# Counting SyncE's issues anew in a planner that orders attention and a feed-forward network

## The chip, the cores and the metric

The kernel runs on one core of one Trainium2 chip. The metric is the device time of one execution in microseconds; three runs before the change gave 1017.01, 1020.22 and 1020.98 us, a median of 1020.22 us. A core has a matrix engine (TensorE, "PE", which loads weights in "PEld"), three engines for elementwise work (VectorE "DVE", ScalarE "ACT", GpSimd "POOL"), and SyncE ("SP"), which in this kernel does nothing but issue DMA transfers, one after the other, and wait for what each of them needs. All of them run their own instruction stream in order and meet at semaphores.

## The reference

```python
# q, k, v: (8 batches, 8 heads, 576 rows, 64), s: (8, 8, 576)
scores = scale * np.matmul(q, k.transpose(0, 1, 3, 2))
cum = np.cumsum(np.maximum(s, 0.0), axis=-1)
bias = -(cum[:, :, :, None] - cum[:, :, None, :])
scores = np.where(causal, -1000000000.0, scores + np.minimum(bias, 0.0))
attn = softmax(scores)                       # row maximum taken off, 1e-9 in the sum
x = (attn @ v) laid out as (4608 tokens, 512)
h = x @ w_in                                 # 512 -> 2048
g = np.where(h > 0.0, h, np.exp(np.minimum(h, 0.0)) - 1.0)
out = g @ w_out                              # 2048 -> 512
```

Causal attention with a bias that decays along the sequence, and behind it a two-layer network with an ELU between the layers.

## The kernel before

**Attention** goes through the heads in pairs (two heads of one batch). The first 320 rows of the first three batches are computed directly in float32 ("low" units). The rest is done with pairs of float16 parts: queries and keys are loaded (`stq`, `stk`), split into a high and a low part (`parts`), written to DRAM (`spread`), and read back in the layout that the score matmuls want (`set`). For each block of 128 queries the scores come out of PE (`sc`, L1141), DVE adds the mask and takes the row minimum (L1144), ACT takes the exponential (L1149), and the weights are scaled and split into float16 parts (L1201 to L1209). A transposed DMA load turns them (`T<-p`, issued on SP by `turned_load`, L481), and the `av` matmuls (L1328) multiply them with the values. A head with four query blocks issues four transposed loads of 4, 6, 8 and 9 blocks of 128 x 128 elements; a head with two blocks issues one joint load, of 9 blocks for the early rows and of 17 for the late ones. The results are written to `x_dram`.

**The feed-forward network** goes through the 4608 tokens in 18 chunks of 256. A chunk's rows are loaded from `x_dram` (`xc`) and split (`xh`, `xl`); the first layer makes `h` (L1503), ACT and DVE make ELU of it (L1515 to L1542), and the second layer adds up `o` (L1560). The first chunk is in float32. The weights are loaded, measured and split in the first part of the run. During the first 60 us PE is kept running with matmuls that nobody reads (`scratch`, the "fillers").

**What sets the order of the work.** The kernel states its operations with what each reads and writes, and a planner (`Plan`) writes out the order at build time. `Plan.run` simulates the five engines: each operation has one or more ways (an engine, a cost in ns, the instructions); of the operations that are ready, the one that can start first names the engine, and on that engine the operation with the earliest due date is taken among those that can start then. The chosen way depends on when the engines come free. A transfer costs SP its issue time and lands later: a fixed lag of 4000 ns, and its bytes at 285 bytes per ns on one shared pipe. `Plan.deadlines` walks the finished order backwards from its end and gives each operation the latest moment at which it could have been done; `Plan.issue` repeats the simulation with those as due dates and keeps the order whose simulated end is earliest. The first round has no due dates and goes by the priorities written in the code. What is kept is then written out, instruction by instruction, and is the order of each engine's queue on the chip. Nothing is chosen anew at run time: an engine waits for its next instruction even where a later one could go.

The issue costs on SP that the simulation uses stand in three constants: `SP_COST` for plain transfers, `SP_SHORT` for the loads and stores around `stq`, `stk`, `spread` and `set`, and `SP_TURN` per block of a transposed load, with a floor in `turned_load`.

Of the kernel before, what the change touches and what calls it, by code (L numbers as in the profile page):

```python
# [35 lines left out]
LAG, RATE = 4000.0, 285.0  # L36
# [6 lines left out]

N_CUT, CUT, N_LOW = 4, 2, 3
PRIO_LOW = 10
SP_COST, SP_SHORT, SP_TURN = 500.0, 640.0, 170.0

N_FREE = 0

# [42 lines left out]


class Op:
    __slots__ = ("ways", "after", "before", "behind", "bufs", "new", "prio", "ready", "left", "filler", "late", "at", "frees")


class Plan:
# [45 lines left out]
    def op(self, prio, ways, reads=(), writes=(), late=()):  # L144

        o = Op()
        o.ways, o.prio, o.filler = ways, (prio, len(self.ops)), False
        o.after, o.before, o.behind, o.bufs, o.new = set(late), [], [], set(), []
        firsts = set()
        for accesses, write in ((reads, False), (writes, True)):  # L150
            expanded = []
            for a in accesses:
                b, part = a if isinstance(a, tuple) else (a, None)
                if not isinstance(b, Piece):
                    expanded.append((b, part))
                elif part is None:
                    known = [key for key in b.whole.parts if key is not None and key[0] == b.label]
                    expanded += [(b.whole, key) for key in known or [(b.label, None)]]
                else:
                    expanded.append((b.whole, (b.label, part)))  # L160
            for b, part in expanded:
                if not b.parts and b not in o.bufs:

                    o.new.append((b, self.place(b)))
                    b.first = o
                firsts.add(b.first)
                if b not in o.bufs:
                    o.bufs.add(b)
                    b.used_by.append(o)
                for key, (writers, readers) in b.parts.items():  # L170
                    if part is None or key is None or key == part:
                        o.after.update(writers)
                        if write:
                            o.after.update(readers)
                writers, readers = b.parts.setdefault(part, ([], []))
                if write:
                    if part is None:
                        b.parts = {None: ([o], [])}
                    else:
                        b.parts[part] = ([o], [])  # L180
                else:
                    readers.append(o)
        o.after.discard(o)
        firsts -= o.after | {o}
        for d in o.after:
            d.before.append(o)
        for d in firsts:
            d.behind.append(o)
        o.left, o.ready, o.late = len(o.after) + len(firsts), {}, 0.0
        self.ops.append(o)  # L190
        return o

# [18 lines left out]
    def deadlines(self, order, end):  # L211

        late = dict.fromkeys(self.ENDS, end)
        for o in reversed(order):
            engine, start, stop, lag = o.at
            t = late.get(engine, end)
            for d in o.before:
                if d.at is not None:
                    t = min(t, d.late - lag - self.HOPS.get((engine, d.at[0]), self.HOP))
            for b in o.bufs:  # L220
                for d in b.followed:
                    t = min(t, d.late - lag - self.HOPS.get((engine, d.at[0]), self.HOP))
            t -= stop - start
            for d in o.behind:
                if d.at is not None:
                    t = min(t, d.late)
            o.late = t
            if engine in late:
                late[engine] = t

    ENDS = ("PE",)
    ROUNDS, WAIT = 8, {"PE": 0.0, "DVE": 0.0, "ACT": 0.0, "Pool": 0.0, "SP": 0.0}

    def issue(self):
        best = None
        for n in range(self.ROUNDS):
            self.reset()
            self.wait = n > 0
            end, order = self.run(False)
            if best is None or end < best[0]:  # L240
                best = end, self.wait, [(o, o.late) for o in self.ops]
            self.deadlines(order, end)
        _, self.wait, lates = best
        for o, late in lates:
            o.late = late
        self.reset()
        return self.run(True)

    def run(self, emit):
# [5 lines left out]
        order = []  # L255
# [6 lines left out]
        def slot_free(key, bufs):  # L262

            held = slots.get(key, ())
            if len(held) < bufs:
                return {}
            was = held[-bufs]
            return None if was.users else was.until
# [5 lines left out]
        while pending:  # L274
# [13 lines left out]
            for o in pending:  # L288
                slots_free = []
                for b, k in o.new:  # L290
                    at = None
                    if b.home_bufs and taken[b.home] == k:
                        b.key, b.bufs = b.home, b.home_bufs
                        at = slot_free(b.key, b.bufs)
# [22 lines left out]
            until, engine = first[0] + (self.WAIT[first[2]] if self.wait else 0.0), first[2]  # L317
            start, _, _, n, o = min(
                (x for x in found if x[2] == engine and (x[0] <= until and not x[4].filler or x is first)),
                key=lambda x: (x[4].late, x[1]))  # L320
            if o.filler:
                start -= GAP
            engine, cost, trace = o.ways[n][:3]
# [1 line left out]
            end = start + cost  # L325
# [36 lines left out]
            at = len(block.instructions)  # L362
# [65 lines left out]
def kernel(  # L428
# [23 lines left out]
    nc = tc.nc  # L452
# [19 lines left out]
    op = plan.op  # L472
    act, dve, pool, pe_ = nc.scalar, nc.vector, nc.gpsimd, nc.tensor

    def load(prio, dst, src, reads, writes, nbytes, late=(), lag=LAG, cost=SP_COST):
        return op(prio, [("SP", cost, lambda: nc.sync.dma_start(dst(), src()), lag, nbytes)],
                  reads, writes, late)

    def turned_load(prio, units, dst, src, reads, writes):

        op(prio, [("SP", max(1330.0, SP_TURN * units), lambda: nc.sync.dma_start_transpose(dst(), src()), LAG,  # L481
                   units * P * P * 2.2)], reads, writes)

    def rounded(prio, n, dst, src, reads, writes, sign=1.0, only=None):

        ways = [
            ("Pool", pool_1(n),
             lambda: pool.tensor_scalar(dst(), src(), sign, 1.0, ALU.mult, ALU.mult)),
            ("ACT", act_s(n),
             lambda: act.activation(dst(), src(), AF.Copy, scale=sign)),  # L490
            ("DVE-SB", dve_1(n),
             lambda: dve.tensor_scalar(dst(), src(), sign, None, ALU.mult)),
        ]
        op(prio, [w for w in ways if only is None or w[0] in only], reads, writes)
# [675 lines left out]
    def halved(u, i, pt, sm, col):  # L1170
# [47 lines left out]
        if joint:  # L1218
            turned_load(prio, 2 * turns - 1, lambda: u.pt.v, lambda: t16.v, used, [u.pt])
        else:  # L1220
            turned_load(prio, turns, lambda: u.pt.v[:, at::n][:, :turns],
                        lambda: t16.v[:, base * P : (base + turns) * P], used, [(u.pt, i)])
# [421 lines left out]
    while rows:  # L1644
        chunk, left = [], TMAX
        while left:
            b, late, r, n = rows.pop(0)
# [82 lines left out]
```

## Time and profile before

| | before |
|---|---|
| median of three runs | 1020.22 us (1017.01 to 1020.98) |
| profiled execution | 1021.47 us, its span 1019.7 us |
| PE busy | 997.2 us (98%) |
| DVE, ACT, POOL busy | 846.5, 660.1 and 261.1 us |
| granted PE clock, mean | 0.998 |
| transfers of SP's queue | 178.45 MB, 76.6% of 16 engines' span |

The span runs from the first to the last instruction. "Busy" is the share of time in which an engine has at least one instruction under way; matmuls are pipelined, so that a busy PE need not run at its full rate. A wait is put down to what came last. In a timeline a row gives the start, the duration, the engine, the line of the kernel, the operation and what it writes and reads. "SPq" is SP's queue, and a duration there is the time that an issue took, not that of the transfer.

### The profile page before, as it was taken

To read this page: it belongs to the slowest core of one execution; us is meant where nothing else is said; L and a number is where in the kernel's file an instruction comes from. 1 tells how busy PE (TensorE), PEld (TensorE's weight loads), DVE (VectorE), ACT (ScalarE), POOL (GpSimd) and SP (SyncE) were. 2 spreads that over 40 slices of the span, in tenths; PEclk is the share of its full clock that TensorE was granted. 3 is DMA by queue.
4 is the path that set the end of the run, shared out by engine and by line. 5 is a ranking of instruction groups with operands and counts; after the bars stand their busy time and mean duration, and the time that the engine had idled before them with its cause. 6 is when DMAs were issued, how large, how long until landed. Compare 5 with 4: busy or idle time off the path is not lost.

```text
span 1019.7 us, 21777 instructions
## 1 busy us (share of the span) xinstructions
PE 997.2 (98%) x7327; PEld 686.5 (67%) x7327; DVE 846.5 (83%) x2352; ACT 660.1 (65%) x1583; POOL 261.1 (26%) x429
## 2 busy tenths in 40 slices
PE   8999999999989999999999999999999999999998
PEld 7677666666656666666666666666766666666665
DVE  6899899989989898999998998898979898744343
ACT  5999776776667676676776777666657665533232
POOL 6332272423232323322222222221412330100000
PEclk9999999999999999999999999999999999999999
DMA  7888743688999997899889999989979998521000
GB/s 205 251 256 274 208 130 87 133 224 162 195 205 205 225 224 178 191 223 214 184 181 225 199 185 203 239 185 240 189 177 217 204 210 180 92 69 43 1 22 21
DMA packets 296724, 179.83 MB, mean 176 GB/s; under 512 B 209908, under 2 KB 270564, under 8 KB 296612
## 3 DMA queue, kind: packets, MB, share of 16 engines
q1 hardware_dynamic: 296612, 178.45, 76.6%
q8 instruction: 57, 0.93, 0.4%
q14 instruction: 55, 0.45, 0.1%
HBM read 93.08 MB, written 36.81 MB: 127 GB/s over the span
## 4 chain that ended last, share of the span: by engine, by line
PE 45%; DVE 4%; DMA 2%; issue 1%; ACT 1%; SPq 0%; DVEq 0%; ACTq 0%
PE h L1503 19%; PE o L1560 19%; PE sc L1141 3%; PE av L1328 3%; DMA T<-p 1%; DVE p L1209 1%; DVE p L1144 1%; DMA stq<-in_qT_dram 0%; DVE gg L1542 0%; DVE h L1535 0%; DMA spread<-parts 0%; ACT p L1149 0%; DVE p L1203 0%; DVE parts L1064 0%; ACT g L1522 0%
## 5 line engine op out<-in xcount | busy, mean ns | idle before, releaser
L1503 PE MATMUL h<-xh,wp 128*128 128x256 f16 x2176 | 401.5, 273 | 0.0
L1560 PE MATMUL o<-wp,gg 128*128 128x512 f16 x1632 | 391.2, 379 | 4.1 <-DVE tops L723 1.5
L1503 PEld LDWEIGHTS <-wp 128*128 128x128 f16 x3264 | 317.4, 98 | 66.1 <-issue 1.3
L1503 PE MATMUL h<-xl,wp 128*128 128x256 f16 x1088 | 296.9, 273 | 0.0
L1560 PEld LDWEIGHTS <-gg 128*128 128x128 f16 x1632 | 156.8, 98 | 152.8 <-DVE gg L1542 5.9
L1149 ACT ACTIVATE p<-p,mn 128x192 f32<-128x192 f32 (+1 forms) x232 | 144.0, 621 | 80.1 <-DVE mn L1144 77.5
L1209 DVE SCALAR_TENSOR_TENSOR p<-p,sm,p 128x512 f16<-128x512 f32 (+3 forms) x258 | 155.1, 630 | 3.4 <-ACT p L1205 1.5
L1515 ACT ACTIVATE g<-h,cs 128x512 f32<-128x512 f32 x136 | 92.4, 679 | 77.1 <-PE h L1503 75.5
L1539 ACT ACTIVATE gg<-h 128x512 f16<-128x512 f32 x127 | 75.4, 593 | 85.5 <-DVE h L1535 84.7
L1542 DVE SCALAR_TENSOR_TENSOR gg<-h,gg 128x512 f16<-128x512 f32 x136 | 93.2, 685 | 25.0 <-ACT gg L1539 24.5
L1141 PE MATMUL sc<-set 128*128 128x288 f16 (+3 forms) x544 | 109.7, 298 | 2.9 <-DVE mn L1144 1.6
L1144 DVE CUSTOM_DVE_ANT_0 p<-sc,maskw 128x192 f32<-128x192 f32 (+1 forms) x232 | 108.6, 480 | 4.2 <-PE sc L1141 1.8
L1535 DVE SCALAR_TENSOR_TENSOR h<-g,cs,h 128x512 f32<-128x512 f32 x136 | 101.9, 749 | 9.1 <-ACT g L1522 5.2
L1201 POOL TENSOR_SCALAR p<-p,sm 128x512 f16<-128x512 f32 (+3 forms) x78 | 53.6, 691 | 217.6 <-DVE sm L1155 80.3
L1205 ACT ACTIVATE p<-p,sm 128x512 f16<-128x512 f32 (+3 forms) x152 | 79.1, 532 | 26.5 <-ACT p L1149 8.3
L1526 DVE TENSOR_SCALAR g<-g 128x512 f32<-128x512 f32 x81 | 36.3, 448 | 58.1 <-ACT g L1515 57.7
L1141 PEld LDWEIGHTS <-set 128*128 128x128 f16 x584 | 55.1, 98 | 35.8 <-issue 6.0
L1328 PEld LDWEIGHTS <-v 128*64 128x64 f16 x960 | 48.5, 111 | 24.4 <-issue 13.7
L1328 PE MATMUL av<-T,v 128*64 128x256 f16 (+5 forms) x960 | 62.3, 281 | 2.1 <-DMA T<-p 2.0
L500 POOL TENSOR_SCALAR v<-va,scales 128x320 f16<-128x320 f32 (+1 forms) x41 | 25.3, 620 | 98.7 <-PE av L1328 66.8
L500 POOL TENSOR_SCALAR xh<-xc,cs 128x512 f16<-128x512 f32 x22 | 16.7, 760 | 130.0 <-PE h L1503 127.0
L1149 ACT ACTIVATION_READ_ACCUMULATOR p<-p,mn 128x1 f32 x232 | 43.6, 188 | 0.0
(205 smaller groups left out, 1271.2 us busy)
## 6 DMA issues: line engine op xcount, KB each, us to landing
set<-spread SPq DMA_DIRECT2D x32, 432.0 KB
spread<-parts_None SPq DMA_DIRECT2D x32, 288.0 KB
set<-spread SPq DMA_DIRECT2D x32, 288.0 KB
raws<-in_w_in_dram SPq DMA_DIRECT2D x16, 512.0 KB
raws<-in_w_out_dram SPq DMA_DIRECT2D x16, 512.0 KB
out_dram<-ost SPq DMA_DIRECT2D x32, 256.0 KB
va<-in_vb_dram SPq DMA_DIRECT2D x16, 352.0 KB
xc<-x_dram SPq DMA_DIRECT2D x22, 256.0 KB
```

The costliest lines, as they stand in the source:

```text
L1141: pe_.matmul(view(sc.v[:, :cw]), l, r, start=n == 0, stop=n == len(pairs) - 1)
L1144: op(prio, [("DVE", 168 + cw + 55 * (i > 0), lambda i=i, sc=sc: dve.tensor_tensor_reduce(pt.v[:, i * cw : (i + 1) * cw], sc.v[:, :cw], mv( ...
L1149: op(prio, [("ACT", 383 + w / 1.2, lambda: act.activation(pt.v[:, :w], pt.v[:, :w], AF.Exp, bias=mn.v[:, n - 1 : n], scale=-1.0, accum_out ...
L1205: ("ACT", 295 + size / 1.2, lambda part=part: act.activation(part(0), own(part), AF.Copy, scale=sm.v[:, r])),
L1209: ("DVE-SB", dve_2(size), lambda part=part: dve.scalar_tensor_tensor(part(1), own(part), sm.v[:, r], part(0), ALU.mult, ALU.subtract)),
L1328: pe_.matmul(av.v[w.h * HB : (w.h + 1) * HB, dst], w.values.v[:, w.h, kb, v], part(w, kb, m), start=kb == 0 and m == 0 and v == 0, stop=kb ...
L1503: pe_.matmul(columns(k), weight_part(f, 0, part)[1]()[:, c * P : (c + 1) * P], xx.v[:, c], start=(c == 0 and m == 0), stop=(c == NCB - 1 a ...
L1515: op(side, [("ACT", act_c(W) + (0 if native else 90), lambda: act.activation(g.v, hp.v, AF.Exp, scale=1.0 if native else by(3)))], [hp] + ...
L1535: op(side, [("DVE", dve_p(W) + 60, lambda: dve.scalar_tensor_tensor(hp.v, g.v, by(2 if sign[0] else 1), hp.v, ALU.mult, ALU.max))], [g, cs ...
L1539: ("ACT", act_c(W), lambda: act.activation(gg.v[:, 0], hp.v, AF.Copy, scale=2.0**-DOWN)),
L1542: op(side, [("DVE", dve_p(W), lambda: dve.scalar_tensor_tensor(gg.v[:, 1], hp.v, 2.0**-DOWN, gg.v[:, 0], ALU.mult, ALU.subtract))], [hp, ( ...
L1560: pe_.matmul(acc[i].v, gg.v[:, g, at], weight_part(f, 1, part)[1](), start=(f == 0 and m == 0), stop=(f == NF - 1 and m == 2),)
```

## The change

Three constants of the planner get other values: the plain issue is counted at 520 ns instead of 500, the transposed load at 195 ns per block instead of 170, and its floor is 1440 ns instead of 1330. `SP_SHORT` stays at 640. The planner makes six rounds instead of eight. In the backward walk, successors that are fillers are left out, and the due date that the choice goes by is kept in a field of its own, `due`, which is copied from `late` after each walk. The operations, the engines that they may run on and SP as the one queue for transfers stay.

```diff
-SP_COST, SP_SHORT, SP_TURN = 500.0, 640.0, 170.0
+SP_COST, SP_SHORT, SP_TURN = 520.0, 640.0, 195.0
...
             for d in o.before:
-                if d.at is not None:
+                if d.at is not None and not d.filler:
                     t = min(t, d.late - lag - self.HOPS.get((engine, d.at[0]), self.HOP))
...
             for d in o.behind:
-                if d.at is not None:
+                if d.at is not None and not d.filler:
                     t = min(t, d.late)
...
-    ROUNDS, WAIT = 8, {"PE": 0.0, "DVE": 0.0, "ACT": 0.0, "Pool": 0.0, "SP": 0.0}
+    ROUNDS, WAIT = 6, {"PE": 0.0, "DVE": 0.0, "ACT": 0.0, "Pool": 0.0, "SP": 0.0}
...
             if best is None or end < best[0]:
-                best = end, self.wait, [(o, o.late) for o in self.ops]
+                best = end, self.wait, [(o, o.due) for o in self.ops]
             self.deadlines(order, end)
+            for o in order:
+                o.due = o.late
...
-                key=lambda x: (x[4].late, x[1]))
+                key=lambda x: (x[4].due, x[1]))
...
-        op(prio, [("SP", max(1330.0, SP_TURN * units), lambda: nc.sync.dma_start_transpose(dst(), src()), LAG,
+        op(prio, [("SP", max(1440.0, SP_TURN * units), lambda: nc.sync.dma_start_transpose(dst(), src()), LAG,
                    units * P * P * 2.2)], reads, writes)
```

More of the change, by code (lines that the diff above doesn't have):

```diff
@@ L94 @@
 class Op:
-    __slots__ = ("ways", "after", "before", "behind", "bufs", "new", "prio", "ready", "left", "filler", "late", "at", "frees")
+    __slots__ = ("ways", "after", "before", "behind", "bufs", "new", "prio", "ready", "left", "filler", "late", "at", "due")
 class Plan:
@@ L188, in op @@
             d.behind.append(o)
-        o.left, o.ready, o.late = len(o.after) + len(firsts), {}, 0.0
+        o.left, o.ready, o.due = len(o.after) + len(firsts), {}, 0.0
         self.ops.append(o)
@@ L240, in issue @@
             if best is None or end < best[0]:
-                best = end, self.wait, [(o, o.late) for o in self.ops]
+                best = end, self.wait, [(o, o.due) for o in self.ops]
             self.deadlines(order, end)
+            for o in order:
+                o.due = o.late
         _, self.wait, lates = best
-        for o, late in lates:
-            o.late = late
+        for o, due in lates:
+            o.due = due
         self.reset()
```

## The prediction

> **What bounds the kernel now.** I read the page's head and table of engines first, then the stretches, to see where TensorE (PE) is idle and what clock it had.
>
> ```profile
> span 1019.7 us, 21777 instructions
> PE 997.2 (98%) x7327; PEld 686.5 (67%) x7327; DVE 846.5 (83%) x2352; ACT 660.1 (65%) x1583; POOL 261.1 (26%) x429
> ...
> 0.00:25.00 25.00, 22.21 (x156) 19.86 (x157) 17.65 (x45) 13.22 (x40) 16.72 (x42) 1.00 0.71 205
> 25.00:50.00 25.00, 22.66 (x162) 15.98 (x160) 21.58 (x81) 22.46 (x71) 8.78 (x23) 1.00 0.86 250
> 50.00:75.00 25.00, 24.65 (x168) 19.30 (x167) 23.46 (x87) 23.13 (x75) 8.87 (x25) 1.00 0.87 255
> ...
> 75.00:150.00 75.00, 74.98 (x396) 50.72 (x394) 68.58 (x178) 60.46 (x147) 27.28 (x45) 1.00 0.69 205
> 150.00:400.00 250.00, 240.37 (x1797) 161.99 (x1797) 229.71 (x678) 174.00 (x437) 79.61 (x116) 1.00 0.86 185
> 400.00:640.00 240.00, 238.65 (x1814) 162.35 (x1812) 219.41 (x629) 168.61 (x414) 61.01 (x95) 1.00 0.94 201
> 640.00:900.00 260.00, 257.98 (x2041) 179.16 (x2040) 221.55 (x587) 165.32 (x352) 57.48 (x82) 0.99 0.87 191
> ...
> 1000.00:1019.70 19.70, 15.71 (x97) 9.24 (x95) 6.59 (x11) 4.80 (x8) 0.00 (x0) 0.96 0.07 27
> ```
>
> The first bracketed column of a stretch is PE's busy time, the column ahead of the DMA share its granted clock. PE is idle 1019.7 - 997.2 = 22.5 us in all: 5.5 in the first 75 us, 9.6 between 150 and 400, 1.4 between 400 and 640, 2.0 between 640 and 900, and 4.0 in the last stretch, where the last output leaves. No order of issues changes PE's work, so a better order can win only idle time and lost clock. Without the last stretch, 18.5 us of idle time are left. How many of them hang on SyncE's queue (SP) is the question, and the view of PE's waits answers it:
>
> ```profile
> PE sc L1141 <- DVE mn L1144: 3.0, 5, 0.8
> PE tr_None L1294 <- ACT psh_None L1166: 2.2, 1, 2.2
> PE scratch L1621 <- POOL ident masks.py:199: 2.1, 1, 2.1
> PE av L1328 <- DMA T<-p: 2.0, 1, 2.0
> PE o L1560 <- DVE tops L723: 1.5, 1, 1.5
> ...
> PE sc L1141 <- DVE pc_None L1227: 1.1, 1, 1.1
> ...
> PE sc_None L1141 <- DMA set<-spread: 0.4, 1, 0.4
> ...
> PE sc L1141 <- DMA kl<-aux: 0.2, 1, 0.2
> ```
>
> Three waits, 2.6 us together, end with a landing; the others end with VectorE (DVE), ScalarE (ACT) or, once, GpSimd. The 2.0 us one is the only stall between 640 and 900, and SP's timeline and the chain of waits show how it came about:
>
> ```profile
> 799.59 0.46 SPq L476 DMA_DIRECT2D out_dram<-ost  x1
> 800.09 0.48 SPq L476 DMA_DIRECT2D stk<-in_kT_dram  x1
> 800.67 0.53 SPq L476 DMA_DIRECT2D x_dram<-x  x1
> 801.31 4.78 SPq L481 DMA_TRANSPOSE T<-p  x1
> 806.14 0.58 SPq L476 DMA_DIRECT2D stk<-in_kT_dram  x1
> ...
> 801.31 8.46 DMA T<-p
> 809.76 0.04 issue
> 809.81 2.54 PE av L1328 x26
> ...
> 829.70 1.41 PE av L1328 x28
> ...
> 800.00:815.00 15.00, 12.98 (x97) 9.23 (x96) 11.48 (x38) 7.96 (x18) 4.46 (x6) 0.89 0.95 197
> ```
>
> SP issues one thing after the other, each about 0.05 to 0.1 us behind the last. The transposed load takes 4.78 us to issue and lands 8.46 us after its start, and the `av` matmuls that need it stand next in PE's order. After the stall the same kind of `av` group takes 2.54 us instead of 1.41: the granted clock of these 15 us is 0.89.
>
> **The change part by part.** No operation is added or removed. What changes is what the planner believes about SP, and so the order that it writes out for all five engines.
>
> *The counts.* By the code a transposed load of u blocks is planned at max(1330, 170 u) ns before and max(1440, 195 u) ns after. A head with four query blocks has u = 4, 6, 8 and 9: 1330 + 1330 + 1360 + 1530 = 5550 ns before, 1440 + 1440 + 1560 + 1755 = 6195 after. A late head with two blocks has one load of 17 blocks: 2890 before, 3315 after. The trace has:
>
> ```profile
> L481 SPq DMA_TRANSPOSE T<-p x138: 1205/1292/4490, 160.9 to 638.7; - x138
> ...
> L481 SPq DMA_TRANSPOSE T<-p x25: 2257/3290/5427, 638.7 to 849.0; - x25
> ...
> 286.27 6.10 SPq L481 DMA_TRANSPOSE T<-p  x4
> ...
> 320.71 6.59 SPq L481 DMA_TRANSPOSE T<-p  x4
> ...
> 445.26 8.27 SPq L481 DMA_TRANSPOSE T<-p  x4
> ...
> 531.85 5.37 SPq L481 DMA_TRANSPOSE T<-p  x4
> ...
> L476 SPq DMA_DIRECT2D xc<-x_dram x46: 370/480/1617, 46.2 to 936.2; - x46
> L476 SPq DMA_DIRECT2D va<-in_vb_dram x44: 328/430/596, 6.7 to 787.7; - x44
> ```
>
> (The three figures are the least, median and largest ns.) The late loads' median of 3290 is hit by the new 3315 and missed by the old 2890. The four quoted heads took 6.6 us on average, 5.37 to 8.27: nearer the new 6.20 than the old 5.55, though the median of one load there, 1292, is below even the old floor. A plain issue of 430 to 480 ns with the 50 to 100 ns behind it fits 520 better than 500. So on the whole the new counts are nearer, most clearly after 640 us. Summed over 32 heads of four loads, 8 of nine blocks (1530 to 1755) and 32 of 17, that is 32 x 0.645 + 8 x 0.225 + 32 x 0.425 = 36.0 us more planned time for SP, and some 300 plain issues at 20 ns add 6.0 us.
>
> *What that gains.* With 0.4 us too little for each late load, SP runs behind the plan by 25 x 0.4 = 10 us over the 25 loads between 639 and 849 us, wherever the plan has no pause in which it catches up. PE's order was written as if transposes landed earlier. A plan that knows better puts other matmuls ahead of the `av` group at 807. I take the whole stall as gone: 2.02 us of idle time (15.00 - 12.98) and (1 - 0.89) x 15 = 1.65 us of clock, together 3.67. Of the two small landing waits I take the 0.4 (`set<-spread`) and leave the 0.2, which falls in the first microseconds.
>
> The Trainium skill ("TensorE: Matmul & The Clock Gate", Part 1) has the clock halve after an idle window of about 3.4 us, the window running free. Here a 2.02 us wait was enough, and the 2.2 us one behind `psh_None` near 292 us kept a clock of 1.00, so the row decides; by a rule under which 2 us never cost clock, the stall is worth 2.0 and not 3.7.
>
> *What is late next.* The new order moves everything. The stalls behind DVE and ACT in 150 to 400 (9.6 us) are small mistimings of in-order engines and get drawn again. The trace of before cannot show the new ones; from below, all 9.6 go (-9.6), from above as many come on top (+9.6). Nothing in the changed constants aims at them, so I take nearly nothing: one new stall of a middling row, the 1.1 us behind `pc_None`.
>
> *Six rounds for eight.* The search keeps the order whose planned end is earliest; two candidates fewer cost nothing if the kept one is among the first six, and otherwise leave a somewhat later one. No row prices it. Bounds: 0 and one landing stall, 3.67; I take 0: the code does not say which round is kept, and six of eight candidates stay.
>
> *Due dates copied, fillers left out.* The copy `due` holds at each choice what `late` held. The fillers read one tile only, `scratch`, so leaving them out changes the due date of its one writer, L1621, which already is PE's first matmul and waits 2.1 us for the identity. Zero, and not hidden behind anything.
>
> *Sum.* The profiled execution took 1021.47 us (1.77 beside its span): 1021.47 - 3.67 - 0.4 + 1.1 = 1018.5. It lies 1.25 above the median of 1020.22; against the median the forecast is **1017.3 us**, 0.3% less. What this kernel's measurement can tell from no change is about 0.5%, 5.1 us, so the forecast is "no change that can be told".
>
> **The rivals.**
>
> *More is won than the one stall.* If late landings also stand behind the DVE and ACT work that releases PE, the 150 to 400 stretch gains too. For: SP is issued back to back there as well, and heads took 5.37 to 8.27 us against 5.55 planned. Against: the waits there are on DVE, ACT and their like. Half of 9.6 and the forecast's 4.07, with no new stall: 1020.22 - 4.07 - 4.8 = 1011.4.
>
> *Nothing moves where it matters.* The 2.0 us stall moves to another transpose, because one load takes up to 5427 ns and any constant misses that: 1020.2. For: its own issue at 4.78 was far above either count. The Trainium skill ("Perfetto Trace Analysis", DMA Instruction, HWDGE) says that the profiled time of an issue covers the lock wait and the making of descriptors; by that, it varies with the traffic and no constant fits. The spread 2257 to 5427 agrees.
>
> *Slower: too high a count for the short loads starves PE in 150 to 400.* There the median load is 1292 ns against 1440 and more planned. The planner holds back attention by up to 0.645 us a head, 20.6 us over the 32 heads, and with it the `x` that the feed-forward chunks need. It decides from the point where this delay is longer than the chunk work that is ready:
>
> ```profile
> 934.64 4.91 PE h L1503 x45
> ...
> 976.32 4.91 PE h L1503 x45
> ```
>
> A chunk is 41.7 us of PE work (the same group of two successive chunks), more than 20.6; but in this stretch few chunks are ready and DVE, busy 229.7 of 250, has to prepare each. Two new stalls of the price of the one above, none gone: 1020.22 + 2 x 3.67 = 1027.6.
>
> **How the numbers follow.** Forecast 0.42; larger gain 0.25; nothing 0.17; slower 0.16. The larger gain gives "faster" 0.25, and 0.06 of the forecast's chance reaches it too; the slower rival gives 0.16 and the no-gain case 0.01. So faster 0.31, same 0.52, slower 0.17. The likeliest case alone spans 1013 to 1021. The range takes in both other sides, down to 1020.2 less the stall and three quarters of the 9.6 (1009) and up to one and a half of the new stalls of the slower rival (1026).
>
> **What would show it.** Right: no wait of `av` on `T<-p` between 640 and 900, the clock at 1.00 there, PE's idle time near 19 us, its busy time per stretch else unchanged, SP's median issue times as before. Wrong on the gain: a wait on `T<-p` elsewhere with a clock below 1. The larger gain would show as more than 244 us of PE in 150 to 400; the slower rival as less than 235 there, with waits on `xc`, `xh` or `gg`. If PE is dense but the span longer, the clock or the tail did it and my account is wrong.

## The result: 0.7% faster

The changed kernel took 1014.79 us (median of 8 runs, 1012.93 to 1017.60), the kernel before 1021.52 us beside it (8 runs, 1017.01 to 1025.13). The ratio is 0.9933, with a 95% interval of 0.9910 to 0.9956: 6.7 us less. The interval leaves out 1, so the change can be told; whether it is beyond the 0.5% that the prediction called the bound of that, the interval leaves open. The forecast was 1017.3 us, 2.5 us too high and inside its range. As a gain it was further off: 2.9 us were forecast and 6.7 measured. The kernel before was 1.3 us slower beside the changed one than in the three runs that the forecast starts from.

A ratio here is an estimate with its own interval and can differ from the quotient of two medians by about 0.1%.

The page's head and the stretches of the changed kernel, with the columns as before (span of the stretch, PE busy, ..., granted clock, DMA share, GB/s):

```profile
span 1014.7 us, 21808 instructions
PE 994.3 (98%) x7335; PEld 686.4 (68%) x7335; DVE 837.8 (83%) x2347; ACT 669.0 (66%) x1594; POOL 252.2 (25%) x419
...
0.00:75.00 75.00, 68.12 (x483) 54.67 (x484) 60.85 (x203) 59.36 (x181) 33.92 (x90) 1.00 0.83 237
75.00:150.00 75.00, 74.58 (x399) 51.14 (x398) 69.58 (x182) 61.79 (x154) 28.92 (x45) 1.00 0.69 207
150.00:400.00 250.00, 243.03 (x1815) 164.19 (x1814) 226.72 (x675) 173.15 (x430) 79.63 (x122) 1.00 0.84 184
400.00:640.00 240.00, 237.82 (x1805) 161.77 (x1804) 216.35 (x627) 172.93 (x418) 62.57 (x92) 1.00 0.95 198
640.00:900.00 260.00, 260.00 (x2070) 180.87 (x2069) 221.53 (x595) 170.02 (x364) 45.77 (x69) 1.00 0.87 193
...
800.00:815.00 15.00, 15.00 (x127) 10.68 (x125) 13.89 (x46) 9.89 (x22) 6.24 (x8) 1.00 0.87 191
```

PE's idle time went from 22.5 to 20.4 us. Between 640 and 900 us it fell from 2.0 to 0.0, and the clock around 807 is 1.00: that stall is gone. Between 150 and 400 it fell from 9.6 to 7.0, between 400 and 640 it rose from 1.4 to 2.2, and in the first 150 us it rose from 5.5 to 7.3. With the 1.65 us of clock these make 2.1 + 1.65 = 3.7 of the 5.0 us by which the spans differ; the remaining 1.3 us lie in PE's busy time, and no row shows them as a wait.

Why the stall went is seen in SP's and PE's timelines. Before, the `av` group stood 6.2 us behind the start of its load's issue (801.31, shown in the prediction):

```profile
807.49 0.30 PE L1328 MATMUL av<-T,v 128*64 128x256 f16 x1
809.81 2.54 PE L1328 MATMUL av<-T,v 128*64 128x256 f16 x27 [2.02 <-DMA T<-p]
```

In the changed kernel it stands 12.5 us behind:

```profile
796.56 4.65 SPq L483 DMA_TRANSPOSE T<-p  x1
...
809.04 1.48 PE L1330 MATMUL av<-T,v 128*64 128x256 f16 x28
```

The issue of the load moved forward by 4.8 us and the group back by 1.6, so most of the room came from the earlier issue.

The largest of PE's waits in the changed kernel:

```profile
PE sc L1143 <- DVE mn L1146: 4.6, 6, 2.6
PE scratch L1623 <- POOL ident masks.py:199: 2.1, 1, 2.1
PE av_None L1289 <- ACT x_None L1342: 2.0, 1, 2.0
PE flat L736 <- DVE tops L725: 1.9, 3, 0.9
PE sc L1143 <- DMA kl<-aux: 1.5, 1, 1.5
PE o L1562 <- DVE gg L1544: 1.1, 2, 0.8
PE av L1330 <- DMA T<-p: 1.0, 2, 0.7
```

The list is of the same kind as before: some ten waits of half a microsecond to 2.6 us, most of them behind DVE and ACT, now at other places. The late transposed loads themselves are as they were:

```profile
L483 SPq DMA_TRANSPOSE T<-p x24: 2254/3364/5077, 644.6 to 848.3; - x24
```

### The profile page after: what moved, and what is told of

Same layout as the page of the kernel before. It is cut to its first block, busy times and chain, and to the rows that moved or that the text cites. A ratio compares the mean times of both kernels' runs of the same rounds, so it can differ in the third digit from the quotient of the medians.

```text
span 1014.7 us, 21808 instructions
## 1 busy us (share of the span) xinstructions
PE 994.3 (98%) x7335; PEld 686.4 (68%) x7335; DVE 837.8 (83%) x2347; ACT 669.0 (66%) x1594; POOL 252.2 (25%) x419
## 4 chain that ended last, share of the span: by engine, by line
PE 78%; DVE 11%; DMA 4%; ACT 3%; issue 2%; SPq 2%; POOL 0%; DVEq 0%; ACTq 0%; POOLq 0%
PE h L1505 28%; PE o L1562 28%; PE sc L1143 8%; PE av L1330 5%; PE h L1501 2%; DVE wp L795 2%; PE o L1555 2%; SPq L478 2%; DMA va<-in_vb_dram 1%; DMA T<-p 1%; DVE p L1211 1%; PE trl L940 1%; PE avl L955 1%; DVE p L1146 1%; DVE gg L1544 1%
## 5 line engine op out<-in xcount | busy, mean ns | idle before, releaser
L1211 DVE SCALAR_TENSOR_TENSOR p<-p,sm,p 128x512 f16<-128x512 f32 (+3 forms) x255 | 150.5, 618 | 2.5 <-ACT p L1207 2.0
L1541 ACT ACTIVATE gg<-h 128x512 f16<-128x512 f32 x134 | 79.5, 594 | 85.0 <-DVE h L1537 83.7
L1544 DVE SCALAR_TENSOR_TENSOR gg<-h,gg 128x512 f16<-128x512 f32 x136 | 93.3, 686 | 25.1 <-ACT gg L1541 24.4
L1203 POOL TENSOR_SCALAR p<-p,sm 128x512 f16<-128x512 f32 (+3 forms) x83 | 59.6, 722 | 217.4 <-DVE sm L1157 117.7
L502 POOL TENSOR_SCALAR v<-va,scales 128x320 f16<-128x320 f32 (+1 forms) x35 | 21.8, 624 | 102.8 <-PE av L1330 97.5
L502 POOL TENSOR_SCALAR xh<-xc,cs 128x512 f16<-128x512 f32 x16 | 11.8, 740 | 139.1 <-PE h L1505 138.2
```

Source lines behind the costliest of these rows:

```text
L1211: ("DVE-SB", dve_2(size), lambda part=part: dve.scalar_tensor_tensor(part(1), own(part), sm.v[:, r], part(0), ALU.mult, ALU.subtract)),
L1541: ("ACT", act_c(W), lambda: act.activation(gg.v[:, 0], hp.v, AF.Copy, scale=2.0**-DOWN)),
L1544: op(side, [("DVE", dve_p(W), lambda: dve.scalar_tensor_tensor(gg.v[:, 1], hp.v, 2.0**-DOWN, gg.v[:, 0], ALU.mult, ALU.subtract))], [hp, ( ...
```

## The experiments

Three of the four parts of the change needed no run. The kernel before with six rounds has the same instruction order on all five engines as with eight, and so has the changed kernel with the old counts back in and eight rounds. The kernel before with only the three new numbers has the order of the changed kernel. So the rounds, the copy `due` and the fillers do nothing here. Everything comes from the three numbers.

Two theories were held against each other. *Better counts*: the plan fits the chip better, so the gain belongs to the values. *Redrawn order*: any other values give another order, and this one happened to be good. A third question was whether the one stall at 807 carries the gain. All ratios below are against the kernel before, run beside each; its medians there were 1022.30 to 1023.01 us.

### The one stall

The kernel before, with one transposed load counted anew only while the kept order is written out:

```diff
+            if (u.b, u.j, u.h, i) == (2, 1, 1, 3):
+                plan.recount = o
...
         self.reset()
+        (e, _, trace, _, size), = self.recount.ways
+        self.recount.ways = [(e, 4780.0, trace, 7000.0, size)]
         return self.run(True)
```

> The kernel before with its own search and due dates; in the order that is written out, one transposed load (third batch, second pair of heads, second head, the late rows: the one of 4.78 us) is counted at 4780 ns and a landing 7000 ns later. Its av group stands 34 matmuls (24 h, 4 sc, 6 o; some 4.4 us of work) later on PE, every other av group where it was. One-stall theory: the wait on T<-p and the low clock at 807 are gone, 3.67 us less than before, ratio 0.9964, and with it over half of the change's gain is explained. Redrawn-order theory: the stall goes here, but the gain of the change is the sum of many small ones, and this kernel is between 0 and 3.7 us faster. If the stall is absent in most executions of the kernel before (the clock's window runs free), the ratio is 1.000.

Measured: 1022.29 us, ratio 0.9985 (0.9967 to 1.0003), some 1.5 us, with an interval from 0 to 3.4 us that does not exclude nothing. The stretches of this kernel:

```profile
152.00:164.00 12.00, 10.12 (x55) 5.83 (x54) 10.98 (x27) 6.38 (x18) 3.98 (x4) 0.86 0.29 69
290.00:302.00 12.00, 9.44 (x58) 5.94 (x57) 9.34 (x21) 8.01 (x21) 5.71 (x6) 0.86 1.07 187
800.00:815.00 15.00, 15.00 (x108) 10.34 (x106) 12.43 (x45) 7.77 (x16) 5.08 (x6) 1.00 1.06 202
815.00:830.00 15.00, 13.09 (x109) 9.02 (x108) 12.65 (x35) 9.00 (x20) 5.58 (x7) 1.00 0.91 195
```

and the same two early stretches of the kernel before:

```profile
152.00:164.00 12.00, 10.14 (x67) 6.32 (x65) 11.86 (x29) 7.20 (x20) 4.80 (x6) 1.00 0.33 74
290.00:302.00 12.00, 9.53 (x60) 5.84 (x61) 11.11 (x28) 9.43 (x25) 6.01 (x6) 1.00 1.11 205
```

The stall at 807 is gone as meant. But two waits on work of DVE came behind it, where the kernel before has none (the line numbers are those of this run's kernel):

```profile
819.54 0.41 PE L1144 MATMUL sc<-set 128*128 128x288 f16 x2 [1.43 <-DVE mn L1147]
827.58 0.41 PE L1144 MATMUL sc<-set 128*128 128x288 f16 x2 [0.48 <-DVE mn L1147]
```

Between 640 and 900 us PE is idle for 2.2 us in this kernel and for 2.0 in the kernel before, so in these executions the idle time moved, and only the clock was won there. The run does not price the stall by itself.

Up to about 800 us the two kernels have the same order, and in the early stretches they have nearly the same idle time (12 - 10.12 and 12 - 10.14; 12 - 9.44 and 12 - 9.53): once with a clock of 0.86, once of 1.00. So whether a wait of this size also costs clock differs from execution to execution. The 1.65 us of clock in the prediction's term may likewise be one execution's; the stall at 807 itself was profiled once only. The pair also shows how far two executions of one order differ: PE's idle time is 5.5 and 6.5 us in the first 150 us, 9.6 and 9.3 between 150 and 400, 1.4 and 2.2 between 400 and 640.

The other way round, in the changed kernel, the same load was counted as nearly free while the order is written out, and its `av` group was taken first among those ready:

```diff
+        self.recount.ways = [(e, 500.0, trace, 500.0, size)]
+        self.early.due = 0.0
         return self.run(True)
```

> The changed kernel with its own search and due dates; in the order that is written out, the same load is counted at 500 ns and a landing 500 ns later, and its av group is taken as soon as the plan thinks it ready: 52 matmuls (36 h, 12 o, 4 sc; some 7 us of work) earlier on PE. One-stall theory: the group stands at about 802 us and its load lands near 805, so PE waits about 3 us and then runs at half clock for 3.4 us: 4.7 us slower than the changed kernel, against the kernel before a ratio of 0.9933 + 0.0046 = 0.998. If a landing stall costs no more than its wait, 0.996. If something later takes the loss back, 0.993.

Measured: 1016.56 us, ratio 0.9926 (0.9900 to 0.9952): no loss against the changed kernel's 0.9933. The row of PE's timeline shows why:

```profile
802.44 1.45 PE L1336 MATMUL av<-T,v 128*64 128x256 f16 x27 [1.22 <-DMA T<-p]
...
795.00:810.00 15.00, 13.78 (x128) 9.91 (x125) 13.04 (x43) 8.11 (x19) 3.97 (x5) 1.00 0.86 186
```

The load landed earlier than I had reckoned, the wait was 1.22 us instead of 3, and the clock stayed at 1.00. So no stall like the one at 807 was put in, and this run cannot price it either.

Neither run settles what the stall is worth. Two orders of the next sections say more: with the transposed loads alone counted anew, and with 641 for 640 at the old counts, PE's idle time between 640 and 900 us is 0.2 and 0.1 us and the clock there is 1.00, as in the changed kernel. Their ratios are 1.0004 and 0.9979. An order without the late stall is thus not enough for 0.9933.

### Each count alone

```diff
-SP_COST, SP_SHORT, SP_TURN = 500.0, 640.0, 170.0
+SP_COST, SP_SHORT, SP_TURN = 500.0, 640.0, 195.0
...
-max(1330.0, SP_TURN * units)
+max(1440.0, SP_TURN * units)
```

> The kernel before with the transposed loads alone counted anew (195 ns a block, floor 1440), plain issues at 500. Better-counts theory: this is the larger correction (36 of 42 us of planned time), so most of the gain is here: ratio 0.994 to 0.996 and no wait on T<-p after 640 us. Redrawn-order theory: anything from 0.993 to 1.003, with stalls in new places; the first 150 us, where no transposed load runs, stay as before (5.5 us of idle time in 0 to 75).

Measured: 1024.12 us, ratio 1.0004 (0.9984 to 1.0025).

```diff
-SP_COST, SP_SHORT, SP_TURN = 500.0, 640.0, 170.0
+SP_COST, SP_SHORT, SP_TURN = 520.0, 640.0, 170.0
```

> The kernel before with the plain issues alone counted at 520 ns, transposed loads as before. Better-counts theory: a small correction (6 of 42 us of planned time), 0.998 to 1.000, and the late loads, still counted at 2890 against a median of 3290, go on stalling PE after 640 us. Redrawn-order theory: anything from 0.993 to 1.003.

Measured: 1024.27 us, ratio 1.0012 (0.9994 to 1.0030). Neither half gains anything, and together they gain 0.67%. With the transposed loads counted anew PE's idle time between 640 and 900 us is nearly gone, as expected, but a wait of 2.4 us for `aux` and one of 2.0 us behind `pc_None` came up instead:

```profile
0.00:75.00 75.00, 67.69 (x469) 53.57 (x470) 60.98 (x205) 57.48 (x180) 33.89 (x90) 0.98 0.78 221
...
640.00:900.00 260.00, 259.81 (x2036) 179.94 (x2031) 219.39 (x581) 164.06 (x352) 55.66 (x75) 1.00 0.83 190
...
PE sc L1141 <- DMA kl<-aux: 2.4, 1, 2.4
...
PE sc L1141 <- DVE pc_None L1227: 2.0, 1, 2.0
```

The `aux` wait lies in the first 75 us, where no transposed load runs and the order is that of the kernel before; yet PE is idle for 7.3 us there with the transposed loads counted anew instead of 5.5, and the wait was 0.2 us before. So part of such differences, too, is one execution's.

With the plain issues alone counted anew, too, no transposed load stalls PE after 640 us, against the expectation. One between 150 and 400 us does, for 1.9 us:

```profile
PE av L1328 <- DMA T<-p: 2.1, 2, 1.9
```

The better-counts theory in its simple form, with parts that add up, fails here, unless the draw of the order hid a gain in both halves.

### Orders drawn anew at the old and the new counts

Five edits change one number by less than one per cent, which no measurement of an issue could justify. At the old counts:

```diff
-SP_COST, SP_SHORT, SP_TURN = 500.0, 640.0, 170.0
+SP_COST, SP_SHORT, SP_TURN = 501.0, 640.0, 170.0
```

> The kernel before with plain issues counted at 501 ns instead of 500, all else as before: nothing is counted better, but the search gives another order. Better-counts theory: the time of before, ratio 0.998 to 1.002. Redrawn-order theory: a new draw, anywhere from 0.992 to 1.004; a ratio below 0.996 or above 1.003 speaks for it.

```diff
-SP_COST, SP_SHORT, SP_TURN = 500.0, 640.0, 170.0
+SP_COST, SP_SHORT, SP_TURN = 500.0, 641.0, 170.0
```

> The kernel before with the loads and stores around stq, stk, spread and set counted at 641 ns instead of 640: a second redraw at the old counts. Better-counts theory: 0.998 to 1.002. Redrawn-order theory: 0.992 to 1.004, and not the same as the redraw with 501.

At the new counts, with 196 ns a block, 521 ns and 641 ns in turn:

> The changed kernel with 196 ns a block instead of 195: a redraw at the new counts. Better-counts theory: keeps the gain, 0.991 to 0.996 against the kernel before. Redrawn-order theory: the gain belongs to the one order, so 0.993 to 1.004 and likely above 0.996.

> The changed kernel with plain issues at 521 ns instead of 520: a second redraw at the new counts. Better-counts theory: 0.991 to 0.996 against the kernel before. Redrawn-order theory: 0.993 to 1.004, likely above 0.996.

> The changed kernel with the loads and stores around stq, stk, spread and set at 641 ns instead of 640: a third redraw at the new counts. Better-counts theory: 0.991 to 0.997. Redrawn-order theory: 0.996 to 1.002.

Measured:

| counts | kernel | us | ratio | 95% interval |
|---|---|---|---|---|
| old | 501 instead of 500 | 1023.53 | 1.0014 | 1.0000 to 1.0028 |
| old | 641 instead of 640 | 1019.94 | 0.9979 | 0.9966 to 0.9991 |
| new | the changed kernel | 1014.79 | 0.9933 | 0.9910 to 0.9956 |
| new | 196 instead of 195 | 1020.20 | 0.9979 | 0.9964 to 0.9994 |
| new | 521 instead of 520 | 1015.99 | 0.9940 | 0.9920 to 0.9960 |
| new | 641 instead of 640 | 1017.01 | 0.9946 | 0.9928 to 0.9964 |

The order with 641 at the old counts, between 640 and 900 us:

```profile
640.00:900.00 260.00, 259.94 (x2061) 179.84 (x2060) 220.57 (x589) 165.89 (x358) 62.74 (x84) 1.00 0.86 193
```

One nanosecond is enough to move the time by 0.2% at the old counts and by 0.46% at the new: the order is redrawn, and that is worth as much as most of the change. Yet the two groups are not alike. With the kernel before as 1, the old counts have a mean of 0.9998, the new ones 0.9950, and only one new order is as slow as the best old one. Better counts had three of the five redraws inside its ranges; it missed 196 at the new counts clearly and 641 at the old ones by a hair.

### Half way, beyond, and the other way

```diff
-SP_COST, SP_SHORT, SP_TURN = 500.0, 640.0, 170.0
+SP_COST, SP_SHORT, SP_TURN = 510.0, 640.0, 182.5
...
-max(1330.0, SP_TURN * units)
+max(1385.0, SP_TURN * units)
```

> The kernel before with counts half way to the new ones: plain 510 ns, 182.5 ns a block, floor 1385. Better-counts theory with a slope: between the two, 0.996 to 0.998. Redrawn-order theory: any of the ratios seen so far, 0.993 to 1.002.

Measured: 1029.28 us, ratio 1.0065 (1.0041 to 1.0088). Two waits for `set`, 5.7 us together, stand out:

```profile
PE sc L1141 <- DVE mn L1144: 6.2, 14, 0.8
PE sc L1141 <- DMA set<-spread: 5.7, 2, 3.8
```

Half way is slower than both the old and the new counts, and outside both ranges expected. Read as a draw of the order, it shows that draws reach over 0.6%.

```diff
-SP_COST, SP_SHORT, SP_TURN = 520.0, 640.0, 195.0
+SP_COST, SP_SHORT, SP_TURN = 540.0, 640.0, 220.0
...
-max(1440.0, SP_TURN * units)
+max(1550.0, SP_TURN * units)
```

> The changed kernel with counts as far beyond the new ones as those are beyond the old: plain 540 ns, 220 ns a block, floor 1550 (a late load 3740 against a median of 3290). Better-counts theory: worse than the changed kernel, as the counts overshoot: 0.996 to 1.002. A theory that PE simply gains from a cautious plan (transfers expected later than they come): as good or better, 0.990 to 0.994. Redrawn-order theory: 0.993 to 1.002.

Measured: 1015.18 us, ratio 0.9930 (0.9907 to 0.9953), no slower than the changed kernel, as the theory of a cautious plan had it.

```diff
-SP_COST, SP_SHORT, SP_TURN = 500.0, 640.0, 170.0
+SP_COST, SP_SHORT, SP_TURN = 480.0, 640.0, 145.0
...
-max(1330.0, SP_TURN * units)
+max(1220.0, SP_TURN * units)
```

> The kernel before with counts as far below the old ones as those are below the new: plain 480 ns, 145 ns a block, floor 1220 (a late load 2465 against 3290). Better-counts and cautious-plan theories: slower than before, 1.002 to 1.008, with more waits on T<-p after 640 us. Redrawn-order theory: 0.995 to 1.002.

Measured: 1036.77 us, ratio 1.0141 (1.0113 to 1.0168), slower than any of the theories had it. The stretches, first with the long counts, then with the short ones:

```profile
150.00:400.00 250.00, 247.25 (x1874) 169.84 (x1873) 230.31 (x671) 178.91 (x440) 74.00 (x118) 1.00 0.89 194
400.00:640.00 240.00, 240.00 (x1826) 164.04 (x1824) 219.30 (x623) 172.21 (x412) 61.30 (x99) 1.00 0.95 204
640.00:900.00 260.00, 259.05 (x2043) 179.37 (x2041) 222.48 (x590) 159.66 (x343) 57.63 (x77) 1.00 0.83 184
```

```profile
150.00:400.00 250.00, 236.51 (x1748) 158.04 (x1748) 226.38 (x661) 167.66 (x424) 84.65 (x118) 0.99 0.85 186
400.00:640.00 240.00, 238.16 (x1810) 162.75 (x1808) 219.61 (x630) 175.62 (x430) 64.66 (x92) 1.00 0.95 193
640.00:900.00 260.00, 250.24 (x1954) 171.37 (x1952) 215.75 (x588) 163.77 (x353) 42.10 (x60) 0.99 0.89 192
```

Between 150 and 900 us PE is idle for 3.7 us with the long counts, 9.2 in the changed kernel, 13.0 in the kernel before and 25.1 with the short ones. The long counts lose some of this again in the first 150 us, where PE is idle for 10.6 us against 7.3 in the changed kernel and 5.5 in the kernel before:

```profile
0.00:75.00 75.00, 66.86 (x468) 53.28 (x469) 62.69 (x199) 56.47 (x175) 34.09 (x89) 1.00 0.82 226
75.00:150.00 75.00, 72.55 (x365) 49.09 (x364) 68.95 (x202) 60.30 (x157) 26.12 (x43) 1.00 0.61 185
```

With the short counts PE waits twice on a transposed load after 640 us, 3.0 us together:

```profile
PE av L1328 <- DMA T<-p: 3.0, 2, 2.0
```

What the two orders at the ends show: the one with too short counts is slower, the one with too long counts is not, even where a count is clearly too long. A late load is counted at 3740 ns beyond, and that kernel's own median is 2976:

```profile
L483 SPq DMA_TRANSPOSE T<-p x22: 2247/2976/4448, 640.4 to 837.7; - x22
```

So nearness to the trace was not needed for the gain: this plan, which expects transfers late, does as well as the one that fits. That it works by PE's order holding more other work ahead of what it waits for is what the code suggests; a kernel that changes only this was not run. Each count stands for one order, and with draws like that half way, the end points make the direction likely (1.0141 against 0.9930, over three times the half-way kernel's distance from 1) and say nothing of its slope.

## Why the prediction was right or wrong

**PE's idle time and lost clock as the only things to win: right in the main.** Idle time between 150 and 900 us is 3.7 us with the long counts and 25.1 with the short ones, and 21.6 us lie between their medians. The signs named for the forecast came: no wait of `av` on `T<-p` between 640 and 900 us, a clock of 1.00 there, and 20.4 us of idle time in all where some 19 were expected. Idle time does not account for everything: PE's busy time also differs, 994.3 against 997.2 us in the changed kernel and the kernel before, of which the clock at 807 explains 1.65.

**The counts: right as counting for the late loads, not shown as the reason.** The new one is nearer there (3364 ns in the changed kernel, 3315 planned), but counts that overshoot do as well.

**The stall at 807: right that it goes, its size open.** In the two profiled executions the whole term of 3.67 us went, with nothing in its place between 640 and 900. The way was only in part the one forecast: matmuls put ahead of the `av` group made 1.6 us of the room, the earlier issue of the load 4.8. Taking the stall out alone gained some 1.5 us (0 to 3.4), but 1.9 us of other waits came behind it, so that is no price of the stall. What the prediction took for granted is that one execution's stall is the kernel's: clock loss behind a like wait, of the size of its 1.65 us, came and went between executions of the same order.

The Trainium skill ("TensorE: Matmul & The Clock Gate", Part 1) says that the activity window runs free, and that the number of slow matmuls at a kernel's start varies by run for that reason. The pairs of 12 us stretches above, with a clock of 0.86 and 1.00 for like waits, agree with a window that runs free; its idle window of some 3.4 us as the condition does not fit, as PE was idle for no more than 1.9 us in the first of them.

**"Nothing in the changed constants aims at" the stalls of 150 to 400: the step that failed.** The term was put at 1.1 us more. They fell by 2.7 us in the changed kernel, where two executions of one order differ by 0.3, and by 6.9 with the long counts (9.6 to 2.75). The rival "more is won than the one stall" had the place right, though not its amount (half of 9.6): its own sign, more than 244 us of PE there, was just missed at 243.03, and its 1011.4 us were 3.4 too low. The objection to it, that these waits end with DVE and ACT and not with a landing, was no objection, as the order of all engines comes from one plan; whether late landings stood behind those waits, no run shows. I had given it 0.25.

**One new stall of 1.1 us: not shown.** 400 to 640 has 0.8 us more and the first 150 us have 1.8 more, but two executions of one order differ by 0.9 and 1.0 there.

**Rounds, due dates, fillers at zero: right.** The orders are the same.

**The nearness of the time: in part luck.** The gain was more than twice the forecast one. The time missed by 2.5 us and not by 3.8, as the gain did, because the kernel before was 1.3 us slower beside the changed one than in its first three runs.

**"Nothing moves where it matters": wrong for this change, right in time for its parts.** Each count alone gave 1.000 and 1.001. With the plain issues alone the stall did turn up at another transposed load (1.9 us).

**Slower by too high counts: did not come.** Even 1550 ns as the floor, 258 ns over that stage's median of 1292 in the kernel before, left PE busier in 150 to 400 (247.25 against 240.37) and not starved. That the 41.7 us of chunk work, which the prediction set against the delay, were the cover is argued and not shown.

What stays open is how much of the 0.67% belongs to the new counts and how much to the draw. Four orders at the new counts lie at 0.9933 to 0.9979, three at the old at 0.9979 to 1.0014, so some 0.5% would be the counts'; the half-way order at 1.0065 says that three or four draws are too few to be sure of it. Nor do the runs separate counts that fit from counts that are merely larger.

## What to carry to other kernels

Where a program is ordered by a simulated plan, judge a change of its costs by several neighbouring values, since one nanosecond may redraw the order and move the time by half a per cent. In this kernel the one order from counts that were too short cost 1.4%, while the one from too long counts cost nothing, so the error to fear here was the short one. And what a stall seen in one profiled execution is worth has to be tested: taken out alone, it let 1.9 us of other waits come in behind it, and a lowered clock like the one that was part of it came and went between executions.

## What was not expected of the hardware

Like waits, 1.9 and 2.5 us of idle time in 12 us, lowered PE's clock to 0.86 in one execution and not in another with the same order up to there, and a wait of 1.22 us left it at 1.00. The wait for the load of `aux` in the first microseconds was between 0.2 and 2.4 us in the traces of these kernels.
